# Sliding-window attention: value products with the exponentials stationary, token-major, and a DMA transpose back

## The chip, the cores and the metric

The kernel runs on one core of one Trainium2 chip. The metric is the device time of that core in microseconds, lower is better; the figure of a kernel is the median of its runs.

## The reference

The input x has 2048 tokens of 1024 features. Two attention blocks with 32 heads of 32 features run on the same x, and a gate mixes them token by token. All tensors are bfloat16.

```python
def _A_ref(x, wqkv, wo):            # linear attention
    q, k, v = split(x @ wqkv)
    pq, pk = phi(q), phi(k)         # phi(t) = where(t > 0, t + 1, exp(t)) + 1e-6
    kv, z = einsum("bhsd,bhse->bhde", pk, v), einsum("bhsd->bhd", pk)
    o = einsum("bhqd,bhde->bhqe", pq, kv) / (einsum("bhqd,bhd->bhq", pq, z) + 1e-6)
    return merge_heads(o) @ wo

def _B_ref(x, wqkv, wo):            # local attention, W = 8 keys, two tokens apart
    q, k, v = split(x @ wqkv)
    idx = pos[:, None] - 2 * arange(8)[None, :]        # the token itself and 7 before it
    logits = where(idx >= 0, q . k[idx] / sqrt(32), -1e9)
    o = einsum("bhsw,bhswd->bhsd", softmax(logits), v[idx])
    return merge_heads(o) @ wo

g = sigmoid((x * gate_w).sum(-1))
return g * A(x) + (1 - g) * B(x)
```

## The kernel before

The tokens are split into even and odd ones (index `e_`, 1024 each), so that the keys of a query are neighbours. Everything stays in SBUF: `xT`, `qT` and `kT` hold x, B's queries and B's keys with the features on the partitions, [128, 8, 2048].

The stages follow each other on TensorE:

1. **V of B**: for each tile of 128 tokens and each half of the features, eight matmuls of 128x512 (`group`, L1326); the result goes from PSUM to a `vst` buffer (`move`, L1357 on VectorE or L1358 on ScalarE) and by DMA to `vB_hbm` (L1379). It goes through HBM because the local part needs windows of tokens that start anywhere.
2. **K and Q of B**, again by `group`, moved to `kT` and `qT` (L1357 to L1361); VectorE keeps a running maximum and minimum of both (`top`, L1287).
3. **K and V of A**, tile by tile: `phi` (L1333 to L1339) writes `pk`, `move` writes `az`, and `state` (L1519) adds the products of a tile to `kva` (L1527).
4. **Q of A**, its normalisation (`over`, L1598 to L1614, which sends reciprocals through `rc_hbm`) and the two output projections; `final` (L1647) multiplies the local result with `B_wo`, and L1651 mixes it with A's and stores it. `qT` is the stationary operand of L1647: the local result has overwritten the queries in place, features on the partitions.

The **local part** is woven into stages 2 and 3. It consists of 18 calls of `fill`, nine for the even and nine for the odd tokens. One fill takes two neighbouring blocks of `nq` = 57 (once 56) queries, `h` = 0 and 1, each with the 64 keys that its windows touch. All 32 heads are done at once. A fill does this:

- two DMAs bring the 64 value rows of each block to a buffer `v` (L1411; ring `vr` of three), partitions 64h to 64h+63;
- **S** (L1418): 64 matmuls, stationary 32x64 of `kT`, moving 32x57 of `qT`, write the scores with keys on the partitions to banks 4 to 7 (`SO`), one bank for each four-head position `j`;
- ScalarE takes the exponential into `E` (L1424), VectorE multiplies it with a 0/1 mask (L1427);
- three slots later (`after(PVLAG, values)`, a slot is one group of eight dense matmuls) **PV**: 64 matmuls (L1437), stationary 64x32 of `v`, moving 64x57 of `E`, write the values with features on the partitions to banks 4 and 5; eight matmuls (L1444) with a block of ones as stationary and 456 columns of `E` moving write the sums, repeated over the 32 features of a head, to banks 6 and 7;
- ScalarE forms the reciprocal of the sums as exp(-ln(s)) (L1453, L1454, buffers `L`), and VectorE multiplies values and reciprocals and writes the result over the queries in `qT` (L1456).

S, PV and the multiplications of one fill use the same four banks, so the next S waits until VectorE has read the last of them.

The order on each engine is not that of the program text. Each operation is given to `P.op` with a cost, the intervals that it reads and writes, and a priority; `schedule` simulates the engines with these costs and writes out one fixed list for each engine. `move` may go to either VectorE or ScalarE ("any"), and the planner picks. DMAs with `"sp"` are issued by SyncE, in the order of its list, and each waits there for its inputs. Waits are semaphores, one for each engine and one for each DMA channel. A second, general path is compiled into the program behind a flag (L1724) and isn't taken here.

Of the kernel before, what the change touches and what calls it, by code (L numbers as in the profile page):

```python
# [6 lines left out]
ACT = mybir.ActivationFunctionType  # L7
ALU = mybir.AluOpType
AX = mybir.AxisListType
BF16 = mybir.dt.bfloat16  # L10
F32 = mybir.dt.float32
I32 = mybir.dt.int32

D = 1024
H = 32
# [1100 lines left out]
def build_kernel(nc, A_x, A_wqkv, A_wo, B_x, B_wqkv, B_wo, gate_w, out):  # L1116
    del B_x
    S = A_x.shape[1]
    NT = S // 128
# [7 lines left out]
    def SB(shape, dtype, name, at=None):  # L1127
        n = SZ[dtype]
        for d in shape[1:]:
            n *= d  # L1130
        if at is None:
            at = base[0]
            base[0] += (n + 31) // 32 * 32
        uid[0] += 1
        h = nc.alloc_sbuf_tensor_at("%s_%d" % (name, uid[0]), list(shape), dtype, offset=at)
        return Tile("S", h, at, list(shape), dtype)
# [14 lines left out]
    ps = ps_guard.__enter__()  # L1151
# [11 lines left out]
            return ps[:, self.i, lo:hi]  # L1163

    banks = [Bank(i) for i in range(8)]
    vB_hbm = nc.dram_tensor("vB_hbm", [S, D], BF16)
    MX = [("M", 0, 1, None)]
    mx_hbm = nc.dram_tensor("mx_hbm", [4, 128], F32)
    rc_hbm = nc.dram_tensor("rc_hbm", [4, H, 4, 512], F32)
# [5 lines left out]
    qT = SB([128, 8, S], BF16, "qT")  # L1175
    kT = SB([128, 8, S], BF16, "kT")
    ws = [SB([128, 8, 1024], BF16, "w%d" % i) for i in range(4)]
    pq0 = SB([128, 8, 512], BF16, "pq0")
    ones = SB([128, 32], BF16, "ones")

    FILLS = [(2 * 57 * b, 57, (0 if b == 0 else 7, 7)) for b in range(8)] + [(2 * 57 * 8, 56, (7, 8))]
    KINDS = ((57, (0, 7)), (57, (7, 7)), (56, (7, 8)))
# [13 lines left out]
    er = Ring([SB([128, 512], BF16, "e%d" % i) for i in range(3)])  # L1196

    ph = base[0]
    vst = Ring([SB([128, 512], BF16, "vst%d" % i) for i in range(8)])
    top_ = base[0]  # L1200
    base[0] = ph
    Er = Ring([SB([128, 32 * 57], BF16, "E%d" % i) for i in range(2)])
    Lr = Ring([SB([128, 8 * 57], F32, "L%d" % i) for i in range(2)])
    vr = Ring([SB([128, 1024], BF16, "v%d" % i) for i in range(3)])
    mtmp = [SB([128, 2, 57], BF16, "mt%d" % i, at=vr.t[2].lo + 256 * i) for i in range(2)]
    base[0] = max(base[0], top_)
    kvT = SB([128, 256], BF16, "kvT")
# [16 lines left out]

    FILL = 0.2
    PVLAG = 3
    SUMS_AT = 3
    WARM = 11
    PASSES = 6
    mm = lambda n: max(n / 2400.0, 0.0267) + 0.0025  # L1230
    act = lambda n: 0.19 + n / 1200.0
    dps = lambda n: 0.14 + n / 960.0

    def plan(seen):

        P = Prog(nc, nc.alloc_semaphore)
# [23 lines left out]
        def C(eng, fn, cost, writes, reads=()):  # L1260
            return P.op(eng, fn, cost, reads=reads, writes=writes, prio=-1)

        C("pool", lambda e: e.memset(ones[:], 1.0), 0.1, [ones.all()])
        C("pool", lambda e: e.memset(eps[:], 1e-6), 0.1, [eps.all()])
        for i, (n, offs) in enumerate(KINDS):
            for h, o in enumerate(offs):
# [87 lines left out]
        def move(dst, src, n, bank, reg, scale=None, reads=()):  # L1354

            if scale is None:
                fd = lambda e: e.tensor_copy(dst, src())  # L1357
                fa = lambda e: e.activation(dst, src(), ACT.Copy)  # L1358
            else:
                fd = lambda e: e.tensor_scalar(dst, src(), scale, None, op0=ALU.mult)  # L1360
                fa = lambda e: e.activation(dst, src(), ACT.Copy, scale=scale)  # L1361
            P.op("any", {"act": fa, "dve": fd}, {"act": act(n) + (0.1 if reads else 0.0), "dve": dps(n)}, reads=[bank.iv] + list(reads), writes=[reg])
# [7 lines left out]
        for t, half in [(4 * b + i, half) for b in range(NT // 4) for half in range(2) for i in range(4)]:  # L1370
            vt, vs = vst.next()
            xs, xr = x_tile(t)
            bank = main.next()
            w, wr = w_half(0, half)
            step = 2 if t == 0 else 8
            for d in range(0, 8, step):
                o = group(bank, xs, w, [xr, ws[0].part((d, d + step), (half * 512, half * 512 + 512))], d, d + step)
            move(vt[:, :], bank.ap, 512, bank, vt.all())
            P.op("sp", lambda e, t=t, vt=vt, half=half: e.dma_start(vB_hbm[t * 128:(t + 1) * 128, half * 512:half * 512 + 512], vt[:, :]), 0.6, reads=[vt.all()],  # L1379
                 writes=[hb(t * 128, (t + 1) * 128, half)], chan="vst%d" % vs, lat=0.5, prio=5)  # L1380
            if (t, half) in early:
                load_w(*early[t, half], after=[o])
# [16 lines left out]
        SO = banks[4:8]  # L1399
# [5 lines left out]
        def fill(e_, qs, nq, offs):  # L1405
            t0 = e_ * HS
            k0 = [qs + nq * h - offs[h] for h in range(2)]
            m = msk[KINDS.index((nq, offs))]
            vt, vslot = vr.next()
            for h in range(2):  # L1410
                P.op("sp", lambda e, h=h: e.dma_start(vt[64 * h:64 * h + 64, :], vB_hbm[t0 + k0[h]:t0 + k0[h] + 64, :]), 0.4,  # L1411
                     reads=[hb(t0 + k0[h], t0 + k0[h] + 64, i) for i in range(2)], writes=[vt.all()], chan="v%d_%d" % (vslot, h), lat=0.5)

            def s_fn(e):
                for c in range(8):
                    for h in range(2):
                        for j in range(4):
                            last = e.matmul(SO[j].ap(c * nq, (c + 1) * nq)[64 * h:64 * h + 64, :], kT[32 * j:32 * j + 32, c, t0 + k0[h]:t0 + k0[h] + 64],  # L1418
                                            qT[32 * j:32 * j + 32, c, t0 + qs + h * nq:t0 + qs + (h + 1) * nq], start=True, stop=True, tile_position=(32 * j, 64 * h))
                return last  # L1420
            P.op("pe", s_fn, 0.55, mode="r", reads=[kT.part((0, 8), (t0 + k0[0], t0 + k0[1] + 64)), qT.part((0, 8), (t0 + qs, t0 + qs + 2 * nq))],
                 writes=[s.iv for s in SO], name="S")
            E, _ = Er.next()
            P.op("act", lambda e: e.activation(E[:, 0:32 * nq].rearrange("p (j q) -> p j q", j=4), ps[:, 4:8, 0:8 * nq], ACT.Exp), act(32 * nq),  # L1424
                 reads=[s.iv for s in SO], writes=[E.all()])
            ev = lambda: E[:, 0:32 * nq].rearrange("p (g q) -> p g q", g=16)
            P.op("dve", lambda e: e.tensor_tensor(ev(), ev(), m[:, :, :].rearrange("p r q -> p (r q)")[:, None, :].to_broadcast([128, 16, 2 * nq]), ALU.mult),  # L1427
                 0.15 + 32 * nq / 1920.0, reads=[E.all(), m.all()], writes=[E.all()])

            def values():  # L1430

                def each(e):
                    def part(c):
                        for j in range(4):
                            for h in range(2):
                                hd = 4 * c + j
                                last = e.matmul(SO[h].ap(c * nq, (c + 1) * nq)[32 * j:32 * j + 32, :], vt[64 * h:64 * h + 64, hd * 32:hd * 32 + 32],  # L1437
                                                E[64 * h:64 * h + 64, (8 * j + c) * nq:(8 * j + c + 1) * nq], start=True, stop=True, tile_position=(64 * h, 32 * j))
                        return last
                    for c in range(SUMS_AT):  # L1440
                        part(c)
                    for j in range(4):
                        for h in range(2):
                            e.matmul(SO[2 + h].ap(0, 8 * nq)[32 * j:32 * j + 32, :], ones[64 * h:64 * h + 64, :], E[64 * h:64 * h + 64, 8 * j * nq:8 * (j + 1) * nq],  # L1444
                                     start=True, stop=True, tile_position=(64 * h, 32 * j))
                    for c in range(SUMS_AT, 8):
                        last = part(c)
                    return last
                P.op("pe", each, 0.61, mode="c", reads=[vt.all(), ones.all(), E.all()], writes=[s.iv for s in SO], name="PV")
                for h in range(2):  # L1450
                    L, _ = Lr.next()
                    n = 8 * nq
                    P.op("act", lambda e, L=L, h=h: e.activation(L[:, 0:n], SO[2 + h].ap(0, n), ACT.Ln), act(n), reads=[SO[2 + h].iv], writes=[L.all()])  # L1453
                    P.op("act", lambda e, L=L: e.activation(L[:, 0:n], L[:, 0:n], ACT.Exp, scale=-1.0), act(n), reads=[L.all()], writes=[L.all()])  # L1454
                    q0 = t0 + qs + h * nq
                    P.op("dve", lambda e, L=L, h=h, q0=q0: e.tensor_tensor(  # L1456
                        qT[:, :, q0:q0 + nq], SO[h].ap(0, n).rearrange("p (c q) -> p c q", c=8), L[:, 0:n].rearrange("p (c q) -> p c q", c=8), ALU.mult), dps(n),
                        reads=[SO[h].iv, L.all()], writes=[qT.part((0, 8), (q0, q0 + nq))])
            after(PVLAG, values)

        pace = [0.0]

        states = []
# [17 lines left out]
        for e_ in range(2):  # L1481
            if True:
                for j in range(8):
                    for isq in range(2):
                        for u in (2 * e_, 2 * e_ + 1):
                            bank = main.next()
                            w, wr = w_cols(1 + isq, j)
# [41 lines left out]
        for t in range(NT):  # L1529
            pkt, _ = pk.next()  # L1530
# [241 lines left out]
```

## Time and profile before

| | |
|---|---|
| median of three runs | 492.45 us (492.34 to 493.23) |
| the profiled execution, its own time | 492.7 us |
| its span, first to last instruction | 490.9 us |
| TensorE busy | 485.7 us (99%), clock granted 1.00 throughout |
| VectorE busy | 274.5 us (56%) |
| ScalarE busy | 166.9 us (34%) |
| DMA | 48.8 MB, mean 99 GB/s |
| dense matmuls of 128x512, L1326 | 1728 in two groups of operands, on 77% of the chain |
| S, L1418 | 2.3% of the chain |
| PV, L1437 and L1444 | 2.0% and 0.7% of the chain |

The profile is of one execution, on the only core. TensorE's busy time is nearly the span, but the busy times of small matmuls overlap and can't be added: what such a batch costs is the distance from its first start to the start of what follows. The chain is the sequence of work that ended last, followed back from the end; its shares by line say on which instructions the span was spent.

### The profile page before, as it was taken

Reading aid. Unit: us, or ns where it says so; the run is one execution under the profiler, and the core shown is the slowest. Engines: PE = TensorE matmul, PEld = TensorE weight load, DVE = VectorE, ACT = ScalarE, POOL = GpSimd, SP = SyncE. Lnnn points to the kernel's source line nnn. Section 1 sums busy time; section 2 is a strip of 40 time slices with the busy share of each in tenths; the row PEclk is TensorE's granted clock in tenths of the full one; section 3 lists DMA queues with packets and bytes.
Section 4 is the critical chain, followed back from the end, with each engine's and each line's share of the span. In section 5 each row is a group of like instructions: output and inputs, shape, how many; then the busy total and the mean of one; then the engine's idle time right before and its main releaser. Section 6 shows DMA issues by size and latency. Waiting matters only on the chain.

```text
span 490.9 us, 11427 instructions
## 1 busy us (share of the span) xinstructions
PE 485.7 (99%) x5123; PEld 226.5 (46%) x5123; DVE 274.5 (56%) x487; ACT 166.9 (34%) x287; POOL 5.1 (1%) x27
## 2 busy tenths in 40 slices
PE   8999999999999999999999999999999999999997
PEld 3444444444444444555454454444444444444443
DVE  2121336899677777465555645596865735334434
ACT  2111121212443344665655556355423323010000
POOL 3000000000000000000000000000000000000000
PEclk9999999999999999999999999999999999999999
DMA  8999993222003045211000100501673406101212
GB/s 208 216 197 271 356 366 100 86 87 85 13 24 109 24 127 146 65 28 43 24 24 24 36 12 4 171 3 22 172 193 80 115 13 180 44 23 45 85 68 89
DMA packets 51069, 48.82 MB, mean 99 GB/s; under 512 B 20161, under 2 KB 38977, under 8 KB 51010
## 3 DMA queue, kind: packets, MB, share of 16 engines
q1 hardware_dynamic: 50322, 47.40, 34.9%
q8 instruction: 42, 0.69, 0.6%
q10 hardware_dynamic: 688, 0.59, 0.4%
q14 instruction: 17, 0.14, 0.1%
HBM read 34.34 MB, written 9.44 MB: 89 GB/s over the span
## 4 chain that ended last, share of the span: by engine, by line
PE 95%; SPq 2%; DVE 2%; DMA 1%; issue 0%
PE ps_all L1326 77%; PE ps_all L1647 11%; PE ps_all L1418 2%; PE ps_all L1437 2%; SPq L1300 1%; PE ps_all L1519 1%; DMA w<-in_B_wqkv_dram 1%; PE ps_all L1444 1%; DVE zsel L1561 1%; SPq L1305 1%; PE ps_all L1598 0%; DVE pq L1339 0%; PE ps_all L1571 0%; DVE e L1337 0%; DVE w L1357 0%
## 5 line engine op out<-in xcount | busy, mean ns | idle before, releaser
L1326 PE MATMUL ps_all<-w,xT 128*128 128x512 bf16 x960 | 213.8, 379 | 0.7 <-DMA xT<-in_A_x_dram 0.6
L1326 PE MATMUL ps_all<-xT,w 128*128 128x512 bf16 x768 | 170.7, 379 | 0.0
L1326 PEld LDWEIGHTS ps_all<-w,xT 128*128 128x128 bf16 x960 | 91.1, 98 | 109.8 <-DMA xT<-in_A_x_dram 2.0
L1326 PEld LDWEIGHTS ps_all<-xT,w 128*128 128x128 bf16 x768 | 73.8, 98 | 89.0 <-issue 1.8
L1647 PE MATMUL ps_all<-w,qT 128*128 128x512 bf16 (+1 forms) x264 | 55.6, 373 | 0.0
L1647 PEld LDWEIGHTS ps_all<-w,qT 128*128 128x128 bf16 x264 | 25.8, 98 | 29.7
L1337 DVE TENSOR_SCALAR e<-e 128x512 bf16<-128x512 bf16 x64 | 18.3, 290 | 34.3 <-ACT e L1335 17.1
L1357 DVE CAST vst<-ps_all 128x512 bf16<-128x512 f32 x15 | 10.4, 691 | 44.3 <-PE ps_all L1326 44.3
L1424 ACT ACTIVATE E<-ps_all 128x1824 bf16<-128x1824 f32 (+1 forms) x18 | 30.4, 1687 | 10.1 <-PE ps_all L1418 9.4
L1335 ACT ACTIVATE e<-ps_all 128x512 bf16<-128x512 f32 x32 | 19.1, 597 | 42.8 <-PE ps_all L1326 42.8
L1427 DVE TENSOR_TENSOR E<-E,msk 128x1824 bf16<-128x1824 bf16 (+1 forms) x18 | 19.8, 1102 | 22.4 <-ACT E L1424 22.4
L1651 DVE SCALAR_TENSOR_TENSOR o<-ps_all,gm,xT 128x512 bf16<-128x512 f32 (+1 forms) x25 | 18.0, 728 | 23.2 <-PE ps_all L1647 22.2
L1333 ACT ACTIVATE e<-ps_all 128x512 bf16<-128x512 f32 x32 | 19.1, 597 | 26.6 <-PE ps_all L1326 25.8
L1358 ACT ACTIVATE vst<-ps_all 128x512 bf16<-128x512 f32 x17 | 10.1, 597 | 49.7 <-PE ps_all L1326 45.5
L1287 DVE TENSOR_TENSOR mx<-mx,kT 128x1024 bf16<-128x1024 bf16 x32 | 20.8, 688 | 9.3 <-ACT kT L1358 9.2
L1287 DVE TENSOR_TENSOR mx<-mx,qT 128x1024 bf16<-128x1024 bf16 x32 | 20.8, 686 | 6.9 <-ACT qT L1361 6.7
L1456 DVE TENSOR_TENSOR qT<-ps_all,L 128x456 bf16<-128x456 f32 (+1 forms) x36 | 21.0, 627 | 6.2 <-ACT L L1454 5.0
L1339 DVE SCALAR_TENSOR_TENSOR pk<-ps_all,e 128x512 bf16<-128x512 f32 x32 | 21.9, 688 | 0.7
L1453 ACT ACTIVATE L<-ps_all 128x456 f32<-128x456 f32 (+1 forms) x36 | 17.8, 547 | 12.4 <-PE ps_all L1437 12.4
L1358 ACT ACTIVATE kT<-ps_all 128x512 bf16<-128x512 f32 x16 | 9.6, 597 | 34.5 <-PE ps_all L1326 34.5
L1361 ACT ACTIVATE qT<-ps_all 128x512 bf16<-128x512 f32 x16 | 9.6, 597 | 31.5 <-PE ps_all L1326 31.5
L1614 DVE TENSOR_TENSOR xT<-xT,rb 128x512 bf16<-128x512 bf16 x24 | 16.2, 688 | 6.6 <-DMA rb<-rc_hbm 6.4
(72 smaller groups left out, 285.6 us busy)
## 6 DMA issues: line engine op xcount, KB each, us to landing
rb<-rc_hbm SPq DMA_DIRECT2D x32, 256.0 KB, 4.8
w<-in_A_wqkv_dram SPq DMA_DIRECT2D x6, 1024.0 KB, 9.3
v<-vB_hbm SPq DMA_DIRECT2D x36, 128.0 KB, 2.8
vB_hbm<-vst SPq DMA_DIRECT2D x32, 128.0 KB, 5.9
w<-in_B_wqkv_dram SPq DMA_DIRECT2D x4, 1024.0 KB, 9.5
xn<-in_A_x_dram SPq DMA_DIRECT2D x16, 256.0 KB, 2.8
out_dram<-o SPq DMA_DIRECT2D x15, 256.0 KB, 2.0
w<-in_A_wo_dram SPq DMA_DIRECT2D x8, 256.0 KB, 3.9
```

The costliest lines, as they stand in the source:

```text
L1287: P.op("dve", lambda e, m=m, op=op: e.tensor_tensor(m[:, 0:n], m[:, 0:n], src, op), 0.08 + n / 1920.0, reads=[m.all(), reg], writes=[m.all()],
L1326: last = e.matmul(bank.ap(), lhs(dc), rhs(dc), start=(dc == 0), stop=(dc == 7))
L1333: P.op("act", lambda e: e.activation(e_[:, :], bank.ap(), ACT.Exp), act(512), reads=[bank.iv], writes=[e_.all()])
L1335: P.op("act", lambda e: e.activation(e_[:, :], bank.ap(), ACT.Exp, accum_out=qe[:, col:col + 1]), act(512) + 0.1, reads=[bank.iv], writes= ...
L1337: P.op("dve", lambda e: e.tensor_scalar(e_[:, :], e_[:, :], 1.0, 1e-6, op0=ALU.min, op1=ALU.add), 0.25, reads=[e_.all()], writes=[e_.all()])
L1339: P.op("dve", lambda e: e.scalar_tensor_tensor(out=dst, in0=bank.ap(), scalar=0.0, in1=e_[:, :], op0=ALU.max, op1=ALU.add), dps(512), read ...
L1358: fa = lambda e: e.activation(dst, src(), ACT.Copy)
L1424: P.op("act", lambda e: e.activation(E[:, 0:32 * nq].rearrange("p (j q) -> p j q", j=4), ps[:, 4:8, 0:8 * nq], ACT.Exp), act(32 * nq), rea ...
L1427: P.op("dve", lambda e: e.tensor_tensor(ev(), ev(), m[:, :, :].rearrange("p r q -> p (r q)")[:, None, :].to_broadcast([128, 16, 2 * nq]), ...
L1456: P.op("dve", lambda e, L=L, h=h, q0=q0: e.tensor_tensor(qT[:, :, q0:q0 + nq], SO[h].ap(0, n).rearrange("p (c q) -> p c q", c=8), L[:, 0:n ...
L1647: last = e.matmul(bank.ap(0, f1 - f0), qT[:, dc, t * 128:(t + 1) * 128], ws[3][:, dc, f0:f1], start=(dc == 0), stop=(dc == 7))
L1651: P.op("dve", lambda e, bank=bank, o_=o_, t=t, n=n, i0=i0, i1=i1, tgt=tgt, c0=c0: e.scalar_tensor_tensor(out=o_[:, i0 * 128:i1 * 128].rear ...
```

## The change

PV is turned round. The masked exponentials become the stationary operand, one head of 57 queries in 64 columns, and the values the moving one. An array tile is now 64 rows by 64 columns, four to the array; `w` = 0 and 1 put 16 heads each on one column half. Each head's values get a 33rd column of ones, so that the same matmul gives the sum of its exponentials. The ones come from memory: `vst` is widened to [128, 16, 33] with the last column set once, and `vB_hbm` and `v` carry it along. The result has queries on the partitions and 8 heads of 33 columns in each of the scores' four banks. VectorE takes the reciprocals of the 16 sums in a row (L1449 of the changed kernel) and multiplies 512 values by them into a buffer `ot` (L1451). Four DMAs for each fill store `ot` to a new tensor `oB_hbm` (L1457), and for each tile of 128 tokens that is complete, a transposing DMA brings it to `qT` (L1462). The steps on ScalarE and the eight matmuls with ones are gone.

```diff
@@ -1163,7 +1163,8 @@
             return ps[:, self.i, lo:hi]
 
     banks = [Bank(i) for i in range(8)]
-    vB_hbm = nc.dram_tensor("vB_hbm", [S, D], BF16)
+    vB_hbm = nc.dram_tensor("vB_hbm", [S, 33 * H], BF16)
+    oB_hbm = nc.dram_tensor("oB_hbm", [S, D], BF16)
     MX = [("M", 0, 1, None)]
     mx_hbm = nc.dram_tensor("mx_hbm", [4, 128], F32)
     rc_hbm = nc.dram_tensor("rc_hbm", [4, H, 4, 512], F32)
@@ -1176,7 +1177,6 @@
     kT = SB([128, 8, S], BF16, "kT")
     ws = [SB([128, 8, 1024], BF16, "w%d" % i) for i in range(4)]
     pq0 = SB([128, 8, 512], BF16, "pq0")
-    ones = SB([128, 32], BF16, "ones")
 
     FILLS = [(2 * 57 * b, 57, (0 if b == 0 else 7, 7)) for b in range(8)] + [(2 * 57 * 8, 56, (7, 8))]
     KINDS = ((57, (0, 7)), (57, (7, 7)), (56, (7, 8)))
@@ -1196,12 +1196,13 @@
     er = Ring([SB([128, 512], BF16, "e%d" % i) for i in range(3)])
 
     ph = base[0]
-    vst = Ring([SB([128, 512], BF16, "vst%d" % i) for i in range(8)])
+    vst = Ring([SB([128, 16, 33], BF16, "vst%d" % i) for i in range(8)])
     top_ = base[0]
     base[0] = ph
     Er = Ring([SB([128, 32 * 57], BF16, "E%d" % i) for i in range(2)])
-    Lr = Ring([SB([128, 8 * 57], F32, "L%d" % i) for i in range(2)])
-    vr = Ring([SB([128, 1024], BF16, "v%d" % i) for i in range(3)])
+    ot = Ring([SB([128, 1024], BF16, "ot%d" % i) for i in range(2)])
+    rs = Ring([SB([128, 16], F32, "rs%d" % i) for i in range(4)])
+    vr = Ring([SB([128, 33 * H], BF16, "v%d" % i) for i in range(3)])
     mtmp = [SB([128, 2, 57], BF16, "mt%d" % i, at=vr.t[2].lo + 256 * i) for i in range(2)]
     base[0] = max(base[0], top_)
     kvT = SB([128, 256], BF16, "kvT")
@@ -1224,7 +1225,6 @@
 
     FILL = 0.2
     PVLAG = 3
-    SUMS_AT = 3
     WARM = 11
     PASSES = 6
     mm = lambda n: max(n / 2400.0, 0.0267) + 0.0025
@@ -1260,7 +1260,8 @@
         def C(eng, fn, cost, writes, reads=()):
             return P.op(eng, fn, cost, reads=reads, writes=writes, prio=-1)
 
-        C("pool", lambda e: e.memset(ones[:], 1.0), 0.1, [ones.all()])
+        for z in vst.t:
+            C("pool", lambda e, z=z: e.memset(z[:, :, 32:33], 1.0), 0.1, [z.part((0, 16), (32, 33))])
         C("pool", lambda e: e.memset(eps[:], 1e-6), 0.1, [eps.all()])
         for i, (n, offs) in enumerate(KINDS):
             for h, o in enumerate(offs):
@@ -1375,8 +1376,8 @@
             step = 2 if t == 0 else 8
             for d in range(0, 8, step):
                 o = group(bank, xs, w, [xr, ws[0].part((d, d + step), (half * 512, half * 512 + 512))], d, d + step)
-            move(vt[:, :], bank.ap, 512, bank, vt.all())
-            P.op("sp", lambda e, t=t, vt=vt, half=half: e.dma_start(vB_hbm[t * 128:(t + 1) * 128, half * 512:half * 512 + 512], vt[:, :]), 0.6, reads=[vt.all()],
+            move(vt[:, :, 0:32], lambda bank=bank: bank.ap().rearrange("p (h d) -> p h d", d=32), 512, bank, vt.part((0, 16), (0, 32)))
+            P.op("sp", lambda e, t=t, vt=vt, half=half: e.dma_start(vB_hbm[t * 128:(t + 1) * 128, half * 528:half * 528 + 528], vt[:, :, :].rearrange("p h d -> p (h d)")), 0.6, reads=[vt.all()],
                  writes=[hb(t * 128, (t + 1) * 128, half)], chan="vst%d" % vs, lat=0.5, prio=5)
             if (t, half) in early:
                 load_w(*early[t, half], after=[o])
@@ -1430,34 +1431,39 @@
             def values():
 
                 def each(e):
-                    def part(c):
-                        for j in range(4):
+                    for i in range(16):
+                        for w in range(2):
+                            hd = 16 * w + i
                             for h in range(2):
-                                hd = 4 * c + j
-                                last = e.matmul(SO[h].ap(c * nq, (c + 1) * nq)[32 * j:32 * j + 32, :], vt[64 * h:64 * h + 64, hd * 32:hd * 32 + 32],
-                                                E[64 * h:64 * h + 64, (8 * j + c) * nq:(8 * j + c + 1) * nq], start=True, stop=True, tile_position=(64 * h, 32 * j))
-                        return last
-                    for c in range(SUMS_AT):
-                        part(c)
-                    for j in range(4):
-                        for h in range(2):
-                            e.matmul(SO[2 + h].ap(0, 8 * nq)[32 * j:32 * j + 32, :], ones[64 * h:64 * h + 64, :], E[64 * h:64 * h + 64, 8 * j * nq:8 * (j + 1) * nq],
-                                     start=True, stop=True, tile_position=(64 * h, 32 * j))
-                    for c in range(SUMS_AT, 8):
-                        last = part(c)
+                                c = 33 * (i % 8)
+                                g_ = 8 * (hd % 4) + hd // 4
+                                last = e.matmul(SO[2 * h + i // 8].ap(c, c + 33)[64 * w:64 * w + nq, :], E[64 * h:64 * h + 64, g_ * nq:(g_ + 1) * nq],
+                                                vt[64 * h:64 * h + 64, hd * 33:hd * 33 + 33], start=True, stop=True, tile_position=(64 * h, 64 * w))
                     return last
-                P.op("pe", each, 0.61, mode="c", reads=[vt.all(), ones.all(), E.all()], writes=[s.iv for s in SO], name="PV")
+                P.op("pe", each, 0.55, mode="c", reads=[vt.all(), E.all()], writes=[s.iv for s in SO], name="PV")
+                o, os_ = ot.next()
                 for h in range(2):
-                    L, _ = Lr.next()
-                    n = 8 * nq
-                    P.op("act", lambda e, L=L, h=h: e.activation(L[:, 0:n], SO[2 + h].ap(0, n), ACT.Ln), act(n), reads=[SO[2 + h].iv], writes=[L.all()])
-                    P.op("act", lambda e, L=L: e.activation(L[:, 0:n], L[:, 0:n], ACT.Exp, scale=-1.0), act(n), reads=[L.all()], writes=[L.all()])
-                    q0 = t0 + qs + h * nq
-                    P.op("dve", lambda e, L=L, h=h, q0=q0: e.tensor_tensor(
-                        qT[:, :, q0:q0 + nq], SO[h].ap(0, n).rearrange("p (c q) -> p c q", c=8), L[:, 0:n].rearrange("p (c q) -> p c q", c=8), ALU.mult), dps(n),
-                        reads=[SO[h].iv, L.all()], writes=[qT.part((0, 8), (q0, q0 + nq))])
+                    r, _ = rs.next()
+                    bv = lambda h=h: ps[:, 4 + 2 * h:6 + 2 * h, 0:264].rearrange("p k (i c) -> p k i c", c=33)
+                    two = [SO[2 * h].iv, SO[2 * h + 1].iv]
+                    P.op("dve", lambda e, r=r, bv=bv: e.reciprocal(r[:, :].rearrange("p (k i) -> p k i", k=2), bv()[:, :, :, 32:33].rearrange("p k i c -> p k (i c)")), 0.2,
+                         reads=two, writes=[r.all()])
+                    P.op("dve", lambda e, r=r, bv=bv, h=h: e.tensor_tensor(
+                        o[:, 512 * h:512 * h + 512].rearrange("p (k i c) -> p k i c", k=2, c=32), bv()[:, :, :, 0:32],
+                        r[:, :].rearrange("p (k i) -> p k i", k=2)[:, :, :, None].to_broadcast([128, 2, 8, 32]), ALU.mult), dps(512),
+                        reads=two + [r.all()], writes=[o.part((512 * h, 512 * h + 512))])
+                q0 = t0 + qs
+                for w, (r0, r1) in [(w, r_) for w in range(2) for r_ in ((0, 48), (48, nq))]:
+                    P.op("sp", lambda e, w=w, r0=r0, r1=r1: e.dma_start(
+                        oB_hbm[q0:q0 + 2 * nq, 512 * w:512 * w + 512].rearrange("(h q) f -> q h f", h=2)[r0:r1], o[64 * w + r0:64 * w + r1, :].rearrange("p (h f) -> p h f", h=2)), 0.5,
+                        reads=[o.all()], writes=[[("O%d_%d" % (w, r0), q0, q0 + 2 * nq, None)]], chan="oo%d_%d_%d" % (os_, w, r0), lat=0.3)
+                while rows[0] < NT and q0 + 2 * nq >= 128 * (rows[0] + 1):
+                    t, rows[0] = rows[0], rows[0] + 1
+                    P.op("sp", lambda e, t=t: e.dma_start_transpose(qT[:, :, t * 128:(t + 1) * 128], oB_hbm[t * 128:(t + 1) * 128, :]), 1.5,
+                         reads=[[("O%d_%d" % (w, r0), t * 128, (t + 1) * 128, None)] for w in range(2) for r0 in (0, 48)], writes=[qT.part((0, 8), (t * 128, (t + 1) * 128))], chan="ot%d" % t, lat=1.3)
             after(PVLAG, values)
 
+        rows = [0]
         pace = [0.0]
 
         states = []
```

## The prediction

> **What bounds the kernel now.** I read the page's busy parts first, then the chain, then TensorE alone around one fill.
>
> ```profile
> span 490.9 us, 11427 instructions
> PE 485.7 (99%) x5123; PEld 226.5 (46%) x5123; DVE 274.5 (56%) x487; ACT 166.9 (34%) x287; POOL 5.1 (1%) x27
> ...
> PEclk9999999999999999999999999999999999999999
> ...
> PE 95%; SPq 2%; DVE 2%; DMA 1%; issue 0%
> ```
>
> TensorE is busy from end to end at full clock and carries 95% of the chain. The rest of the chain is the first 15 us of loads and 0.5 us of DVE at the end. So a microsecond counts only if it comes out of TensorE's own stream, or opens a hole in it. The chain's shares by line in the trace are L1418 2.3% (scores, S), L1437 2.0% and L1444 0.7% (values and row sums, PV): of 490.9 us these are 11.3 and 13.3 us, or 0.63 and 0.74 us for each of the 18 fills. TensorE in order of time shows a fill directly (start, length, group):
>
> ```profile
> 150.35 0.70 PE L1418 MATMUL ps_all<-qT,kT 32*64 32x57 bf16 x64
> 150.99 5.35 PE L1326 MATMUL ps_all<-xT,w 128*128 128x512 bf16 x24
> 156.27 0.28 PE L1437 MATMUL ps_all<-E,v 64*32 64x57 bf16 x24
> 156.37 0.37 PE L1444 MATMUL ps_all<-E,ones 64*32 64x456 bf16 x8
> 156.56 0.51 PE L1437 MATMUL ps_all<-E,v 64*32 64x57 bf16 x40
> 157.00 3.20 PE L1326 MATMUL ps_all<-xT,w 128*128 128x512 bf16 x14
> ```
>
> The lengths overlap; starts are what to subtract. S holds the engine for 150.99 - 150.35 = 0.64 us, PV for 157.00 - 156.27 = 0.73 us. Single starts, over all fills, give 0.632 and 0.725 us. Inside the batch at 304.15 us the first 32 pairs of weight load and matmul go about 3 ns apart; the 33rd matmul starts 0.239 us in, and from there a pair goes every 8.3 ns to the 64th. PV has the same shape: start again after 0.23 us (the sums, 190 ns of streaming, lie over this gap), then 40 pairs at 8.3 ns with one hiccup of 0.05 us. From the last matmul to the next batch's first load there are 0.139 us after S and 0.127 us after PV.
>
> The other engines have room. Around the local part:
>
> ```profile
> 186.00:311.00 125.00, 125.00 (x2671) 63.26 (x2671) 70.09 (x124) 71.55 (x106) 0.00 (x0) 1.00 0.14 36
> ```
>
> The columns are PE, PEld, DVE, ACT, POOL, clock, DMA share, GB/s: no hole in TensorE, DVE and ACT under 60%, DMA 14%.
>
> **What the Trainium skill says.** "TensorE: Matmul & The Clock Gate", in its opening table, gives TensorE a queue of 64 instructions. The trace agrees: 32 pairs, which are 64 instructions, are fast. Its Part 1 has matmul starts never closer than about 25 ns; within one array tile the trace agrees (the 33-column state matmuls, L1519, follow each other on their tile every 25.4 ns), while different tiles start 2 to 4 ns apart. Its "LDWEIGHTS" section prices a load at columns/1.2 ns, 47.5 ns for 57 columns. The trace says less: loads of 64 columns last 102 ns against 89 ns for 32, 0.41 ns a column, and in S a tile takes a new 64-column load and matmul every 32.5 ns. I use the trace, and keep 47.5 ns as the bad end. "TensorEngine Tiling (Array Packing)", section Tiling Modes, lists 64x64 as four tiles and 64x32 as eight, and says that a change of mode drains the engine; the 0.127 to 0.139 us above are that drain, and remain.
>
> **The change, part by part.** Line numbers are of the kernel before.
>
> *PV on TensorE.* Before: 64 matmuls and 8 ones-matmuls. After: 64 matmuls, 57 stationary columns, 33 moving, the sums coming with column 33. The nearest row is S: 64 pairs, almost as wide a load. First 32 pairs over four tiles are eight turns. I put a turn at 32.5 - 7 x 0.41 = 29.6 ns, so 0.24 us, as long as the queue's gap. The other 32 pairs arrive every 8.3 ns, 33 ns per turn of four, slower than the tile. So 0.239 + 31 x 0.0083 = 0.496 us to the last start, plus a drain of 0.136: 0.632 us, against 0.725. 18 x 0.093 = **-1.67 us**. Below this it hardly can go, because arrival binds; above, see the first rival.
>
> *Order on TensorE.* As built, the local stretch has 40 departures from the dense matmuls instead of 39 (four states stand alone instead of three), and three PV stand directly behind a state instead of two. A stretch of 8 dense matmuls lasts 1.834 us, of 16 3.560, so each departure costs 2 x 1.834 - 3.560 = 0.108 us; PV behind a state took 0.763 instead of 0.725. Together **+0.15 us**.
>
> *ACT* loses L1453 and L1454, 36 x (0.545 + 0.584) = 40.6 us; none of it on the path.
>
> *DVE* loses L1456, 36 x 0.624 = 22.5 us, and gains 36 multiplies of 512 at 0.69 us (the 512-element rows from PSUM) and 36 reciprocals of 16. The one such row, from SBUF, took 0.241 us; from PSUM I allow 0.2 to 0.4. Net +11 us (up to +17). As built, 7 of the az moves (L1357, 0.69) go to ACT: net +6 us in 185 us. What can cost is the wait of the next S for the banks. Before, after the PV at 200.85, DVE finished at 204.39 and S came at 205.44. After, the work between is 2 x 0.24 + 2 x 0.69 plus handover, some 2.2 us, where before it was 2.8; but in places two e/pk pairs and a kva addition (0.29, 0.69, 0.43) are put between, 3.6 us, and the closest S stands 16 dense matmuls (3.56 us) behind PV. I take **+0.1 us**, bounds 0 and 1.5 (0.2 us at half of the 17 gaps).
>
> *SP and DMA.* 72 stores of oB at 0.45 us of issue and 16 transposes at 1.29 us (L1300) are 53 us more on SP's queue between about 133 and 318 us. The transposes wait there for their stores to land (2 to 4 us by rows of that size), and the v loads (L1411) queue behind. But a v load goes out once the PV three fills earlier is done, and has two fills, about 20 us, against 2.6 us to land. The transposed result is read first by L1647 at 418 us, 100 us after the last fill. About 8.4 MB more DMA go into a stretch that is 14 to 24% busy. Rows of V grow from 64 to 66 bytes per head, 3% of what L1379 and L1411 move. DMA has no spare before 63 us, but the first K weights are issued at 38.0 us, land in at most 11.4, and are used at 62.3. Eight small memsets on POOL stand ahead of the first store at 11.0 us; POOL finishes all its start-up work in 4.6 us. All these I cost at **0**, hidden by that slack; bounds 0 and 1.
>
> The sum is -1.67 + 0.15 + 0.1 = **-1.4 us**: a span of 489.5 instead of 490.9, or 491.3 for the profiled execution instead of 492.7. That execution lies 0.25 us above the median of 492.45, so I forecast 491.0 us.
>
> **Rivals.**
> 1. *The four tiles bind, slower.* Only four tiles share the work where eight did. PV gets no shorter once a turn reaches about (0.725 - 0.136)/16 = 36.8 ns. At the page's 47.5 ns it is 0.02 + 16 x 0.0475 + 0.136 = 0.92 us, +0.195 each, +3.5 us: 496.2 with the +0.25 of order and waits. Load and stream in series (24 + 14 + overhead) lie between, about 493. Against it: S renews 64 columns in 32.5 ns, and L1519 shows loads running under streams in the same rows. For it: S splits its loads over four row groups, PV only over two. Chance 0.13.
> 2. *DVE's lateness gives it back, no change.* S waits for the second multiply after most fills: 0.08 us x 17 eats the gain, 492.3. For it: the interleaved pairs above. Against it: the 1 us of slack seen before and ACT's two steps gone. Chance 0.18.
> 3. *The chip does not do fewer things*: 72 pairs to 64 saves nothing if the pace after the gap is worse with loads from E. S already loads from arbitrary odd offsets of kT at 8.3 ns, so I include this in the 0.13.
>
> **Numbers.** The likeliest case, 0.69, has 490.3 to 491.5 as its own range. A measurement of this kernel can tell about 0.2%, 1 us: faster 0.68, same 0.19, slower 0.13. The range 489.9 to 493.3 takes in the second rival, the bounds of DVE and DMA and half-way cases of the first, and leaves out its full price.
>
> **What would show it.** PV batches, start to next start, near 0.63 us with a pair every 8.3 ns in the second half; gaps before S unchanged at about 0.42 us on PEld; ACT's share near 26%; DVE near 57%; PE still without a hole between 63 and 418 us. I am wrong if PV lasts 0.7 us or more, if dense matmuls stall before S, or if L1647 waits for a transpose.

## The result, and the profile after

The changed kernel's median is 490.28 us (489.84 to 490.38, four runs) against 492.57 us (492.34 to 493.23, four runs, the profiled one included): a ratio of 0.995, 95% interval 0.9932 to 0.9967. The forecast was 491.0 us, range 489.9 to 493.3. Measured again in the experiments below, five runs against seventeen, it was 490.32 against 492.31 us, ratio 0.9963 (0.9949 to 0.9976).

The page of the changed kernel, the lines that answer to those of before; L1440 is now PV, L1419 S, L1451 the multiplication, L1457 the store to `oB_hbm`:

```profile
span 488.6 us, 11209 instructions
...
PE 476.1 (97%) x4912; PEld 225.1 (46%) x4979; DVE 275.3 (56%) x514; ACT 137.9 (28%) x224; POOL 5.5 (1%) x34
...
PE 94%; issue 2%; DVE 2%; DMA 1%; ACT 1%; SPq 0%; DVEq 0%
...
L1451 DVE TENSOR_TENSOR ot<-ps_all,rs 128x512 bf16<-128x512 f32 x36 | 23.6, 683 | 0.0
...
oB_hbm<-ot SPq DMA_DIRECT2D x36, 96.0 KB, 2.0
```

TensorE is still the bound. The 97% is not idle time: in this execution the record of one dense matmul behind many batches is missing (4912 matmuls for 4979 weight loads), and the chain calls the gap "issue". A second execution of the same kernel has them; its stretch around the local part (columns PE, PEld, DVE, ACT, POOL, clock, DMA share, GB/s) shows TensorE full, ScalarE down from 71.55 to 51.33 us, VectorE where it was, and DMA up from 14% to 37%:

```profile
186.00:311.00 125.00, 125.00 (x2493) 62.35 (x2491) 70.04 (x145) 51.33 (x64) 0.00 (x0) 1.00 0.37 89
```

TensorE in order of time, in the same second execution, around one fill:

```profile
146.06 0.81 PE L1419 MATMUL ps_all<-qT,kT 32*64 32x57 bf16 x64
146.81 5.35 PE L1327 MATMUL ps_all<-xT,w 128*128 128x512 bf16 x24
152.09 0.68 PE L1440 MATMUL ps_all<-v,E 64*57 64x33 bf16 x64
152.70 0.60 PE L1327 MATMUL ps_all<-xT,w 128*128 128x512 bf16 x2
```

PV holds the engine for 152.70 - 152.09 = 0.61 us, where it was 0.73; over all 18 fills the median is 0.611 us, from the first weight load to the first one of what follows. The S shown takes 0.75 us instead of 0.63: it has a hole, a stretch of 0.11 us in which nothing starts, near its end, behind the 62nd of its 64 pairs. Such holes come back below.

Where the span of the profiled pair went: the first S starts at 125.61 instead of 126.49 us, -0.9. From there it takes 194.63 instead of 195.90 us, -1.3, to the first `fold`, the matmuls with `kvT` that follow the local part (L1571 before, L1577 after). The rest is alike. In the -1.3, the 18 PV are 11.0 us instead of 13.1 (-2.1), one more departure from the dense matmuls costs 0.1, and holes in three S batches and one state batch cost 0.8. In the pair of executions taken later, the same stretch is 194.21 against 196.02 us, -1.8, with holes of 0.32 and 0.18 us. Without the holes both pairs say about -2.0 us.

### The profile page after: what moved, and what is told of

Read it like the earlier page. It is cut to its first block, busy times and chain, and to the rows that moved or that the text cites. A ratio compares the mean times of both kernels' runs of the same rounds, so it can differ in the third digit from the quotient of the medians.

```text
span 488.6 us, 11209 instructions
## 1 busy us (share of the span) xinstructions
PE 476.1 (97%) x4912; PEld 225.1 (46%) x4979; DVE 275.3 (56%) x514; ACT 137.9 (28%) x224; POOL 5.5 (1%) x34
## 4 chain that ended last, share of the span: by engine, by line
PE 94%; issue 2%; DVE 2%; DMA 1%; ACT 1%; SPq 0%; DVEq 0%
PE ps_all L1327 77%; PE ps_all L1653 11%; PE ps_all L1440 2%; PE ps_all L1419 2%; DMA xT<-in_A_x_dram 1%; PE ps_all L1525 1%; DVE zsel L1567 1%; ACT e L1334 0%; PE ps_all L1604 0%; DVE pq L1340 0%; SPq L1301 0%; PE ps_all L1577 0%; SPq L1306 0%; DVE e L1338 0%; ACT kT L1359 0%
## 5 line engine op out<-in xcount | busy, mean ns | idle before, releaser
L1327 PE MATMUL ps_all<-w,xT 128*128 128x512 bf16 x922 | 207.4, 379 | 4.9 <-issue 3.0
L1327 PE MATMUL ps_all<-xT,w 128*128 128x512 bf16 x746 | 167.4, 379 | 2.6 <-issue 2.1
L1338 DVE TENSOR_SCALAR e<-e 128x512 bf16<-128x512 bf16 x64 | 18.0, 284 | 42.4 <-ACT e L1334 25.2
L1653 PEld LDWEIGHTS ps_all<-w,qT 128*128 128x128 bf16 x264 | 25.8, 98 | 29.6
L1359 ACT ACTIVATE az<-ps_all 128x512 bf16<-128x512 f32 x24 | 14.4, 601 | 41.8 <-PE ps_all L1327 41.8
L1451 DVE TENSOR_TENSOR ot<-ps_all,rs 128x512 bf16<-128x512 f32 x36 | 23.6, 683 | 0.0
```

What stands on the lines that cost most here:

```text
L1327: last = e.matmul(bank.ap(), lhs(dc), rhs(dc), start=(dc == 0), stop=(dc == 7))
L1338: P.op("dve", lambda e: e.tensor_scalar(e_[:, :], e_[:, :], 1.0, 1e-6, op0=ALU.min, op1=ALU.add), 0.25, reads=[e_.all()], writes=[e_.all()])
L1451: P.op("dve", lambda e, r=r, bv=bv, h=h: e.tensor_tensor(o[:, 512 * h:512 * h + 512].rearrange("p (k i c) -> p k i c", k=2, c=32), bv()[:, ...
L1653: last = e.matmul(bank.ap(0, f1 - f0), qT[:, dc, t * 128:(t + 1) * 128], ws[3][:, dc, f0:f1], start=(dc == 0), stop=(dc == 7))
```

## The experiments

Theory A: a batch of small matmuls lasts as long as its pairs of weight load and matmul take to arrive at TensorE; PV got shorter because it has 64 pairs instead of 72. The traces do not show the queue itself; what they can show is whether the starts keep one pace whatever the shape, so that the count alone sets the length. Rivals: B, the new tiles and streams are what counts; C, it is the work of ScalarE and VectorE between PV and the next S; D, a part of the measured gain is chance of the start.

### The kernel before without the matmuls with ones

```diff
                     for c in range(SUMS_AT):
                         part(c)
-                    for j in range(4):
-                        for h in range(2):
-                            e.matmul(SO[2 + h].ap(0, 8 * nq)[...], ones[...], E[...], ...)
                     for c in range(SUMS_AT, 8):
...
-                    P.op("act", ... SO[2 + h].ap(0, n), ACT.Ln), ...)
+                    P.op("act", ... SO[2 + h].ap(0, n), ACT.Ln, bias=eps[:, :], scale=0.0), ...)
```

> The kernel before, with only the eight matmuls with ones left out of each PV (the sums are left out with them: the logarithm reads a constant in their place, with the same two steps on ScalarE). Values stay feature-major, 64x32 tiles, everything else as before. Theory A (a PV lasts as long as its pairs of weight load and matmul take to arrive): 64 pairs instead of 72, so PV falls from 0.725 us to about 0.62 (0.239 + 31 x 0.0083 + 0.122), 18 x 0.1 = -1.9 us in the local stretch, S unchanged at 0.632; the total falls by about as much as the changed kernel's does. Rival B (the turned tiles or the shorter stream are what saves): PV stays above 0.69, total within 0.5 us of before. Rival C (the work of ScalarE and VectorE between PV and the next S is what counts): no change, since those steps are all here.

```profile
155.72 0.68 PE L1437 MATMUL ps_all<-E,v 64*32 64x57 bf16 x64
156.33 3.84 PE L1326 MATMUL ps_all<-xT,w 128*128 128x512 bf16 x17
```

PV, still 64x32 tiles with values stationary, lasts 156.33 - 155.72 = 0.61 us, 0.608 over all fills. The total is 489.85 us against 492.31, ratio 0.9953 (0.9939 to 0.9967), at least as far below as the changed kernel with its 0.9963. B and C fall: with the old tiles, the old layout and both steps on ScalarE, leaving out eight matmuls gives the whole gain. What the change does for TensorE is that the sums come without matmuls of their own.

### Short streams for the ones

The pairs stay 72, but the eight with ones stream 57 columns instead of 456. As in the run before, the logarithm reads a constant, since the sums are not complete.

```diff
-                            e.matmul(SO[2 + h].ap(0, 8 * nq)[...], ones[...], E[64 * h:64 * h + 64, 8 * j * nq:8 * (j + 1) * nq],
+                            e.matmul(SO[2 + h].ap(0, nq)[...], ones[...], E[64 * h:64 * h + 64, 8 * j * nq:8 * j * nq + nq],
...
```

> The kernel before with the eight matmuls with ones kept, but each streaming only the first 57 columns instead of 456 (the sums are incomplete; the logarithm reads a constant). Tells what of the 0.116 us between the PV before (0.725) and the PV without ones (0.609) is the eight pairs and what their long streams. Arrival alone: 8 pairs x 8.3 ns on top of 0.609, 0.675 us. If the 190 ns of streaming cost nothing because they lie over the gap in arrivals: 0.725 as before.

```profile
155.39 0.28 PE L1437 MATMUL ps_all<-E,v 64*32 64x57 bf16 x24
155.49 0.21 PE L1444 MATMUL ps_all<-E,ones 64*32 64x57 bf16 x8
155.62 0.52 PE L1437 MATMUL ps_all<-E,v 64*32 64x57 bf16 x40
156.07 0.61 PE L1326 MATMUL ps_all<-xT,w 128*128 128x512 bf16 x2
```

156.07 - 155.39 = 0.68 us; 0.675 over the fills. So the 0.117 us between the PV before and the PV without ones are two things: 0.067 us are eight pairs at 8.3 ns, and 0.050 us are the long streams. In one PV of the kernel before, no matmul starts from 0.124 to 0.289 us, while the long streams run, although weight loads go on from 0.230 us; then a burst starts, and after the 56th pair comes one more gap, from 0.416 to 0.475 us. With short streams the starts go on from 0.224 us, that second gap is gone, and all 40 pairs follow at 8.3 ns. The long streams were therefore not free, although they lay over the first gap. How they cause the second gap is not shown. The one run took 491.37 us, 0.9 below the one run of the kernel before that was taken with it; 18 x 0.05 is 0.9.

### More and fewer pairs

```diff
-                    for i in range(16):
+                    for i in range(12):                               # 48 pairs
+                    for i in list(range(16)) + [8, 9, 10, 11]:        # 80 pairs
```

> The changed kernel with 48 instead of 64 matmuls in PV (eight heads left out). Theory A: 16 pairs less at 8.3 ns, PV 0.611 - 0.133 = 0.48 us. A proportional price would give 0.75 x 0.611 = 0.46 with the drain and 0.375 + 0.111 = 0.49 without; so this alone does not tell, but it fixes the price of a pair.

> The changed kernel with 80 matmuls in PV (eight heads done twice, same result). Arrival: 16 pairs x 8.3 ns more, 0.611 + 0.133 = 0.744 us. If a batch of more than 64 pairs meets another gap, as the hole of 0.05 us near the 57th pair of the PV before suggests: about 0.79 us.

TensorE's weight loads with 48 pairs, and its matmuls with 80:

```profile
151.82 0.45 PEld L1440 LDWEIGHTS ps_all<-v,E 64*57 64x57 bf16 x48 [0.42 <-DVE mx L1288]
152.30 0.33 PEld L1327 LDWEIGHTS ps_all<-xT,w 128*128 128x128 bf16 x3
```

```profile
152.33 0.81 PE L1440 MATMUL ps_all<-v,E 64*57 64x33 bf16 x80
153.08 0.60 PE L1327 MATMUL ps_all<-xT,w 128*128 128x512 bf16 x2
```

PV is 0.477, 0.611 and 0.744 us with 48, 64 and 80 pairs: 0.13 us for 16 pairs both times, 8.3 ns each, and no gap beyond 64 as long as all streams are short. The single runs, 488.00 and 492.93 us, lie 2.3 below and 2.6 above the changed kernel's 490.32; 18 x 0.133 is 2.4. With 80 pairs PV is longer than the PV before (0.744 to 0.725).

### Load width and stream length

```diff
-  e.matmul(SO[...][64 * w:64 * w + nq, :], E[..., g_ * nq:(g_ + 1) * nq], vt[..., hd * 33:hd * 33 + 33], ...)
+  e.matmul(SO[...][64 * w:64 * w + 32, :], E[..., g_ * nq:g_ * nq + 32], vt[..., hd * 33:hd * 33 + 33], ...)   # 32 columns loaded
...
+  e.matmul(SO[...][64 * w:64 * w + nq, :], E[..., g_ * nq:(g_ + 1) * nq], vt[..., v0:v0 + 64], ...)            # 64 columns moving; v0 = 33 * min(hd, 30)
```

> The changed kernel with only 32 of the 57 query columns loaded as stationary (25 queries of a block are left out). Theory A (arrival of instructions binds from the 33rd pair on): the first 32 pairs turn faster, 25 to 26 ns a turn instead of 29.6, but the second half keeps its 8.3 ns and PV stays at 0.59 to 0.62 us. Rival B (a tile's load and stream bind): PV falls by 16 turns x 4 ns or more, to 0.54 or less.

> The changed kernel with 64 instead of 33 value columns moving in each matmul of PV (neighbouring heads' columns along, overwriting each other in PSUM, so the local result is not the reference's). Theory A: a 64-column stream is 26.7 ns and still fits under the arrival of a turn (33 ns): PV grows only by the longer last stream, 31 x 0.417 = 13 ns, to about 0.62. Rival B (load and stream of one tile follow each other): each of 16 turns grows by 13 ns, PV 0.82.

```profile
151.75 0.56 PEld L1440 LDWEIGHTS ps_all<-v,E 64*32 64x32 bf16 x64 [0.42 <-DVE mx L1288]
152.34 0.33 PEld L1327 LDWEIGHTS ps_all<-xT,w 128*128 128x128 bf16 x3
```

```profile
152.07 0.60 PEld L1441 LDWEIGHTS ps_all<-v,E 64*57 64x57 bf16 x64 [0.42 <-DVE mx L1288]
152.71 0.33 PEld L1327 LDWEIGHTS ps_all<-xT,w 128*128 128x128 bf16 x3
```

0.588 and 0.637 us over the fills. A turn is one round over the four tiles. With the narrow load the first turns come every 25.2 ns instead of 29.5, and the second half keeps its 8.3 ns: PV falls by 23 ns, where rival B asked for 16 x 4 or more. With nearly twice the stream, a turn is 30.7 ns and PV grows by 26 ns, not by the 16 x 13 of rival B, but by twice the 13 that A gave it; about half of it lies before the last start and half after. So the widths move PV by 4% and do not set its time. The tiles are the slower part only at first: a batch of the changed kernel runs at their pace to about the 48th pair, and follows the 8.3 ns from there on. The single runs took 489.97 and 490.71 us.

### The order over the tiles

```diff
-                    for i in range(16):
-                        for w in range(2):
-                            hd = 16 * w + i
-                            for h in range(2):
+                    for w in range(2):
+                        for h in range(2):
+                            for i in range(16):
+                                hd = 16 * w + i
```

> The changed kernel with PV's order turned: 16 matmuls one after another on the same tile, then the next tile, instead of going round the four. Same 64 pairs, same result. If only the number of pairs counted, PV would stay at 0.61. If a tile needs its turn of about 29.6 ns, as the first half of the batch shows, PV becomes 64 x 29.6 ns + 0.11 = 2.0 us, and the whole 18 x 1.4 = 25 us slower: the four tiles in rotation are then what lets arrival be the bound.

```profile
154.18 1.70 PEld L1440 LDWEIGHTS ps_all<-v,E 64*57 64x57 bf16 x64 [0.42 <-DVE mx L1288]
155.90 0.55 PEld L1327 LDWEIGHTS ps_all<-xT,w 128*128 128x128 bf16 x4
```

155.90 - 154.18 = 1.72 us, and 509.76 us in the one run, 19.4 more than the changed kernel's 490.32. Within a tile the starts are 28 to 30 ns apart, as the first half of the normal batch showed; two or three matmuls overlap at each change of tile, which is what the 2.0 us left out. So the count of pairs sets the time only while the tiles are taken in turn: four tiles at 29.5 ns can take a pair every 7.4 ns, just faster than the 8.3 ns at which pairs arrive.

### Without the way back, and with late transposes

```diff
-                for w, (r0, r1) in ...:
-                    P.op("sp", ... oB_hbm[...], o[...] ...)
-                while rows[0] < NT and ...:
-                    P.op("sp", ... dma_start_transpose(qT[...], oB_hbm[...]) ...)
```

> The changed kernel without the stores to oB and without the transposing DMAs (the local result does not reach the output; qT keeps the queries). If the way back is hidden, as costed at 0: the total is within 0.3 us of the changed kernel, PV 0.61. If DMA traffic delays TensorE's instructions (the holes of 0.1 to 0.5 us seen after three S and inside one state batch of the changed kernel): these holes go, some 0.7 us less than the changed kernel.

```diff
-                while rows[0] < NT and q0 + 2 * nq >= 128 * (rows[0] + 1):
-                    ...dma_start_transpose...
...
         while todo or later or states:
             slot(1.0)
+        for t in range(NT):
+            P.op("sp", lambda e, t=t: e.dma_start_transpose(...), ...)
```

> The changed kernel with all 16 transposes put behind the last fill (same result; TensorE's order is the same). The holes inside batches of the local stretch summed to 0.77 and 0.32 us in the two profiles of the changed kernel and to 0.04 us without the way back. If transposes in flight delay TensorE's instructions: the holes fall to 0.1 us or less and the total is 0.2 to 0.5 us below the changed kernel. If the stores do it, or the holes are chance: 0.1 to 0.8 us of holes as before, total within 0.3 us of the changed kernel. The risk: 16 x 1.25 us of transposes on SP's queue up to about 335 us, where the first reciprocals of A are sent; a stall there would cost up to 1 us.

Without the way back the kernel takes 490.31 us, with it 490.32: hidden, as costed. The holes in S and state batches of the local stretch sum to 0.04 us there, but the total did not fall by the 0.7 us that the holes of the profiled changed kernel add up to. With late transposes the holes are 0.40 us and the total 490.28 us. So the transposes do not make the holes.

The largest hole, in a state batch of the profiled changed kernel (L1525, L1519 before), follows no wait that the profile shows:

```profile
194.69 0.17 PEld L1525 LDWEIGHTS ps_all<-az,pk 128*32 128x32 bf16 x16
195.26 0.17 PEld L1525 LDWEIGHTS ps_all<-az,pk 128*32 128x32 bf16 x16 [0.40 <-issue]
```

Whether the stores make such holes is not settled: over the profiles, holes in that stretch sum to at most 0.18 us in five without stores (the kernel before twice, and variants) and to 0.11 to 0.77 us in eight with them, which overlap. DMA traffic at the moment is not needed for a hole in S: during eight of the S batches with holes, two of them of the kernel before, no DMA packet was in flight.

A second kind of delay outside the stretch is a wait, and adds to what single executions differ by. The version without the way back stands still for 0.56 us at 350 us, before the sums of A's normalisation (L1595 there, L1598 before):

```profile
349.35 0.69 DVE L1611 TENSOR_TENSOR pq<-pq,rb 128x512 bf16<-128x512 bf16 x1 [0.49 <-DMA rb<-rc_hbm]
349.96 0.68 DVE L1340 SCALAR_TENSOR_TENSOR xT<-ps_all,e 128x512 bf16<-128x512 f32 x1
350.70 0.61 PE L1595 MATMUL ps_all<-xT,zsel 128*32 128x512 bf16 x8 [0.49 <-DVE xT L1340]
```

VectorE waits there for the reciprocals that come back from `rc_hbm` by DMA, and so writes the last part of `xT` late; TensorE starts 0.05 us after that. In ten of the thirteen profiles TensorE waits for VectorE at one or two of these places, up to 0.87 us long, in both profiles of the kernel before too. The change does not touch this stage.

### Both kernels again

> The changed kernel again, for the parts that may differ from one execution to the next. Theory D (0.9 us of the 2.3 gained in the profile lie ahead of the first S and are chance of the first loads): the first S starts anywhere between 125.5 and 126.6 us, as it does in the other kernels of this call, and the holes after S and in the state batch are at other places or absent. Rival: the start belongs to the change, first S at 125.6 again, and the holes are at the same places. PV 0.61 in both.

> The kernel before again: first S at 126.5 us again if its later start belongs to the kernel, anywhere between 125.5 and 126.6 if it is chance. PV 0.725, no holes. The ratio to itself shows what the comparison can tell: 1.000 with an interval of about 0.002 either way.

The start of TensorE, the kernel before, in the profile of the prediction and in the later one:

```profile
6.49 1.96 PE L1326 MATMUL ps_all<-w,xT 128*128 128x512 bf16 x8 [0.36 <-DMA xT<-in_A_x_dram]
8.71 7.57 PE L1326 MATMUL ps_all<-w,xT 128*128 128x512 bf16 x33 [0.26 <-DMA xT<-in_A_x_dram]
```

```profile
5.71 2.14 PE L1326 MATMUL ps_all<-w,xT 128*128 128x512 bf16 x8 [0.18 <-DMA xT<-in_A_x_dram]
8.04 8.23 PE L1326 MATMUL ps_all<-w,xT 128*128 128x512 bf16 x37 [0.18 <-DMA xT<-in_A_x_dram]
```

The first dense matmuls wait for x and start 0.8 us apart in two executions of one kernel. The first S of the kernel before is at 126.49 and 125.63 us, of the changed kernel at 125.61 and 125.88, of the version with late transposes at 126.61. D holds: the 0.9 us ahead of the first S in the profiled pair are chance. Of the holes, the rival was half right: in the changed kernel two of three S holes and the one in a state batch come at the same places again, smaller in the state batch (0.47, then 0.12 us); the kernel before, for which none were expected and which had none in its first profile, now has two in S. The kernel before against itself gave 0.9998 (0.999 to 1.0006).

## Why the prediction was right, point by point

- **The bound.** Right: only TensorE's own stream counted. ScalarE lost 29 us of work, VectorE gained 1 us, DMA 8.7 MB, and none of it moved the end. One reading was incomplete: besides the first 15 us and the last 0.5, the chain of before also runs through VectorE for some 7 us between 319 and 326 us, a stage that the change does not touch.
- **PV, -1.67 us: right mechanism, too small; -2.1 measured.** The pace was right: first turns of 29.5 ns (I had 29.6), then 8.3 ns, the last start at 0.500 us (0.496). That the last start agrees so well is partly luck: the start of the 33rd pair, which I took from S as 0.239 us, is not the same for all batches; it was 0.224 without the ones, 0.216 with the narrow load and 0.258 here, where the tiles are still behind. The term mis-sized is the drain, from the last matmul to the next load, taken from S as 0.136 us: it is 0.111. About 10 of these 25 ns are the shorter last stream, an estimate from the run with 64 columns moving, whose 31 columns more made the drain 11 ns longer; with 57 columns and the old tiles it was 0.124. Why S, on 32x64 tiles, drains longer than that is not shown. The 25 ns of drain, less 4 ns by which the last start came later, make 18 x 0.02 = 0.4 us.
- **Order, +0.15 us: +0.11.** The extra departure is there, 0.108 us. The 0.04 us more for a PV behind a state are not: three such PV last 0.610 us, where the two of before took 0.763, so this gave back 0.08 us, counted in the -2.1, in place of costing.
- **DVE's wait, +0.1 us: nothing.** The reciprocals took 0.248 us from PSUM, the multiplications 0.680; the last multiplication of a fill ended at least 1.07 us before the next S, against 1.05 before. The sum behind the worst case does not add up: with two e/pk pairs and a kva addition between, its own parts give 4.6 us and not 3.6, which is the sum for one pair. From PV's first load to the last multiplication it took 2.3 to 2.4 us in most fills, 3.4 in four, and 5.0 in one whose next S came 7.6 us after PV.
- **SP and DMA, 0: right.** Transposes landed in 3.4 us, stores in 2.0, and leaving both out changed nothing. The last transpose was in place at 322 us, and the first matmul that reads it came at 416.
- **The rivals.** The four tiles do not bind in rotation; out of it they do, and the kernel is then 17 us slower than the one before. The Trainium skill's price for a weight load ("TensorE: Matmul & The Clock Gate", section LDWEIGHTS), columns/1.2 ns or 47.5 ns for 57 columns as an estimate from it, is not what any run shows: 28 to 30 ns from start to start on one tile, with the load in it. DVE's lateness did not come. That fewer pairs might save nothing was wrong in the other direction: they saved more than their arrival.
- **Not foreseen.** The 0.05 us that long streams cost in each PV before; the prediction saw the hiccup and didn't ask for its cause. TensorE was to be without a hole between 63 and 418 us, and was not: the local stretch of the profiled execution has 0.8 us of them. And in the profile that the forecast starts from, the first S came 0.9 us later than in the profile after; that difference belonged to neither kernel. The size of the change is about -2.0 us (490.32 against 492.31), between the forecast of -1.4 and the first measurement of -2.3; all the terms that were off, drain, order and wait, were off on the same side. The 490.28 us measured first lie just outside the 490.3 to 491.5 of the likeliest case.
- **Shares.** ScalarE is at 28%, not 26. Its two steps overlapped in pairs, so they held 36.8 us of busy time (17.8 and 19.0) and not 40.6, and the planner gave it two moves of K and Q besides the seven of V of A. VectorE is at 56%, not 57, with 1 us more and not 6; its new steps overlap in pairs too. Neither share has a part in the time.

## What to carry to other kernels

When TensorE is full and small tiled matmuls are woven into dense ones, price a batch by its number of load and matmul pairs, not by columns. Here it was about 0.24 us for the first 32, 8.3 ns for each further one, 0.11 to 0.14 us of drain by shape, and 0.11 us more for each departure from the dense matmuls. To save there, let an operand carry what would need matmuls of its own (a column of ones for the sums), and take the tiles in turn. Compare profiles stage by stage over two executions before a microsecond at the start or in a single hole is put down to the change.

## What the runs showed of the hardware

- The first 32 pairs of a batch went 2 to 4 ns apart on different tiles. Further ones came every 8.3 ns, whatever the tile shape (32x64, 64x32 or 64x64), the load (32, 57 or 64 columns) or the stream (33, 57 or 64 columns).
- Eight matmuls streaming 456 columns in the middle of such a batch caused a second gap of 0.05 us; with 57 columns there was none, nor with 80 pairs of short streams.
- A 64-row tile renewed 57 stationary columns and streamed 33 in 29.5 ns, 32 columns and 33 in 25.2 ns, 57 and 64 in 30.7 ns. Load and stream of one tile overlap: 31 columns more to stream cost 1.2 ns a turn, where streaming them takes 13 ns, an estimate from the 512- and 256-column matmuls of L1647 before (379 and 272 ns, 0.42 ns a column).
- From the last matmul of a tiled batch to the next load it took 0.111 us with 33 columns streaming, 0.122 with 64, and 0.124 with 57 on 64x32 tiles.
- Holes of 0.02 to 0.5 us without a wait that the profile shows appear inside batches of small matmuls, in both kernels and often at the same places of the program; their cause stays open.
